# A retention + gated-convolution kernel: half of the last convolutions moved off TensorE, and the first two steps re-ordered

## The chip, the cores and the metric

The kernel runs on one core of a Trainium2 chip. The core has five engines that work beside each other, each on its own queue of instructions in a fixed order: TensorE (PE, with its weight loads shown as PEld), VectorE (DVE), ScalarE (ACT), GpSimd (POOL) and SyncE (SP, which here only issues transfers). An instruction starts when it is at the head of its queue and the semaphores it waits for have come. The metric is the device time of the launch in microseconds; less is better. The kernel before takes 191.95 us, the median of four runs (190.09 to 192.88).

## What is computed

Two stages, batch 8, 8 heads of 64, sequence 576, model width 512:

```python
# stage 1: retention, per head h with its decay gamma[h]
scores = scale * (q @ k.T)
ret    = scores * where(i >= j, gamma[h] ** (i - j), 0)
x      = (ret @ v), heads side by side           # (8, 576, 512)
# stage 2: gated unit with a causal depthwise convolution of 5 taps
gate_pre[:, t, d] = sum_k conv_w[k, d] * x[:, t + k - 4, d]
out = (sigmoid(gate_pre) * (x @ w_val)) @ w_out
```

## The kernel before, in words

**Stage 1.** The sequence of each batch element is cut into two chunks of 256 and a remainder of 64. A *step* is one 256-chunk of one element, or the remainders of two elements together; there are 20 steps, s0 to s19. The order of steps is such that a remainder step comes two steps after its pair or directly after it; the last step, s19, is a remainder. For a step, `load` brings k, q and v as f32 by SP (512 KB each for a full step), `cast` multiplies k and q with their decay factors and casts all three to bf16 (tiles `kb`, `qb`, `vb`; lines 231 and 238, on POOL except in the first two steps), `transp` turns `kb` and `qb` on PE and ACT and DVE copy the results to `kt` and `qt` (lines 251, 259, 261), `scores` makes `sc` (278) which DVE masks into `am` (285), `state` and `state_sum` keep the running state (302, 318, 320, with the bf16 copy `w` at 322), `inter` and `values` sum the step's output into the PSUM tile `o` (340, 353), and `evac` copies `o` into the stage's output `xt`, one half by DVE and one by ACT. The loads run up to four steps ahead of the step that uses them and the casts two.

**Stage 2.** When enough of `xt` is there, `push_block` (395) puts a *block* of up to 512 columns on the list `work`. The 12 blocks are, in order: two of 256 (b0), one of 512 each for b1, b2, b3, one of 256 with four remainders, 512 each for b4, b5, b6, and then two of 256 (b7) and the last four remainders. So blocks 8 to 11 have 512, 256, 256 and 256 columns. A block consists of four tiles of 128 channels (d = 0 to 3) and of these jobs:

- `conv(0)` and `conv(2)` (413): the convolution of two tiles each, as 40 matmuls with diagonal 64 x 64 weights (`diag`, made at the start by `prep_diag`, line 183), into two PSUM tiles `cps`; ACT makes the gates `gt` with a sigmoid (426);
- four `val(d)` (429): four matmuls with `w_val` into `vps` (434), then DVE multiplies with the gate into `zt` (436);
- `outp(m)` (438) for each 128 rows: four matmuls with `w_out` into `ops` (441), ACT copies to `ob` (444), SP stores it (450).

`fill(us)` takes jobs from the front of `work` while a credit lasts, so that stage 2 fills PE between the dependent pieces of stage 1. The jobs of blocks b0 (its first half) and b4 leave their `outp` on the list `late` until the next block comes.

**Order.** Nothing is scheduled automatically. Each step runs through a list of codes written out by hand: `FIRST` for s0, `SECOND` for s1, `FULL[0]` and `FULL[1]` for the other full steps, `PART` for remainders. In them `Sa`, `Sb` are scores of two head pairs each, `I` inter, `Va`, `Vb` values, `T` the transposes of the next step, `X` and `XS` the next step's state, `E` evac, `B` push_block, a number is a `fill`. In `FIRST` the step is done in two halves a and b (`first`, 477): `Ca:kD` casts half a of k on DVE, `Ca:qP` half a of q on POOL, `D2:D` and `D0:P` are `prep_diag` on DVE and POOL, `C1`, `C2` cast the steps s1 and s2, `WV`, `WO` cast the weights. After s19 the rest of `work` is emptied: this *tail* (blocks 8 to 11) has only stage 2 in it, and its `vps` and `ops` tiles take the PSUM buffers of stage 1.

Of the kernel before, what the change touches and what calls it, by code (L numbers as in the profile page):

```python
# [31 lines left out]
def kernel(  # L32
# [10 lines left out]
    nc = tc.nc  # L43
    ctx.enter_context(tc.manual_schedule())
    B, H, S, D = q.shape
    DM = moe_w_val.shape[0]
    P = 128
# [4 lines left out]
    HP = H // 2  # L52
    DT = DM // P
    KC = moe_conv_w.shape[0]
    PAD = KC - 1
    assert D == HF and DM == H * D and REM == HF and B % 2 == 0
    scale = 1.0 / math.sqrt(D)
# [1 line left out]

    TPS, DSS, CAP = False, False, 2.0  # L60
    PB, EV, TE = [4, 2, 2], "DA", "AD"
    C1, LO = "PDP", "1vo23"
    SPL, REMD = 0, [2, 0, 2, 0]
    cst = ctx.enter_context(tc.tile_pool(name="cst", bufs=1))
    ld = ctx.enter_context(tc.tile_pool(name="ld", bufs=4))
    cs = ctx.enter_context(tc.tile_pool(name="cs", bufs=4))
    at = ctx.enter_context(tc.tile_pool(name="at", bufs=3))
    sp = ctx.enter_context(tc.tile_pool(name="sp", bufs=4))
    xp = ctx.enter_context(tc.tile_pool(name="xp", bufs=2))
    gl = ctx.enter_context(tc.tile_pool(name="gl", bufs=6))  # L70
    zp = ctx.enter_context(tc.tile_pool(name="zp", bufs=2))
    os_ = ctx.enter_context(tc.tile_pool(name="os", bufs=4))
    PS = bass.MemoryType.PSUM
    scp = ctx.enter_context(tc.tile_pool(name="scp", bufs=PB[1], space=PS))
    opp = ctx.enter_context(tc.tile_pool(name="opp", bufs=PB[2], space=PS))
# [81 lines left out]
    cw = cst.tile([P, KC, DT], F32)  # L157
# [10 lines left out]


    xtb = []  # L170
    for i in range(2):
        xt_ = cst.tile([P, DT, 2, PAD + NSC * SC], BF16, tag=f"xt{i}", name="xt")
        nc.vector.memset(xt_[:, :, :, 0:PAD], 0.0)
        xtb.append(xt_)
# [43 lines left out]
    def cast(s):  # L218
        u, bb, n = steps[s]
        r = st[s]  # L220
        R = 1 if bb is None else 2
        shp = [P, R, H, D]
        f0 = n * 2
        nb = 2 if bb is None else 4
        kb = cs.tile(shp, BF16, tag=f"kb{R}", name="kb", bufs=nb)
        qb = cs.tile(shp, BF16, tag=f"qb{R}", name="qb", bufs=nb)
        vb = cs.tile(shp, BF16, tag=f"vb{R}", name="vb", bufs=nb)

        how = C1 if s == 1 else "PPP"
        for e, dst, src, f in ((how[0], kb, r["kf"], fk), (how[1], qb, r["qf"], fq)):  # L230
            (nc.vector if e == "D" else nc.gpsimd).tensor_tensor(  # L231
                dst, src.rearrange("p h r d -> p r h d"),
                f[:, f0:f0 + R, :].unsqueeze(3).to_broadcast(shp), op=ALU.mult)
        vsrc = r["vf"].rearrange("p h r d -> p r h d")
        if how[2] == "A":
            nc.scalar.copy(vb, vsrc)
        else:
            nc.gpsimd.tensor_copy(vb, vsrc)  # L238
        r.update(qb=qb, kb=kb, vb=vb)

    def transp(s, which="kq"):
        if s >= NS:
            return
        r = st[s]
        R = 1 if steps[s][1] is None else 2
        for nm in which:
            src = r[nm + "b"]
            tp = (scp if TPS else glp).tile([P, HP, R, P], BF16, tag="sc" if TPS else "gps", name="tp" + nm)
            for hp in range(HP):
                for rr in range(R):  # L250
                    nc.tensor.transpose(tp[:, hp, rr, :],  # L251
                                        src[:, rr, 2 * hp:2 * hp + 2, :].rearrange("p a d -> p (a d)"), ident)
            t = at.tile([P, HP, R, P], BF16, tag=f"{nm}t{R}", name=nm + "t")
            copy(TE[nm == "q"], t, tp)
            r[nm + "t"] = t

# [102 lines left out]
    def evac(s):  # L359
        u, bb, n = steps[s]  # L360
        r = st[s]
        R = 1 if bb is None else 2
        o = r["o"]
        if bb is None:

            if u % 2 == 0:
                xrs[u // 2] = xp.tile([P, DT, 4, PAD + REM], BF16, name="xr")
            xr = xrs[u // 2]
            j0 = 2 * (u % 2)
            nc.gpsimd.tensor_copy(xr[:, :, j0:j0 + 2, 0:PAD], xts[u][:, :, :, NSC * SC:NSC * SC + PAD])  # L370
            for x in range(2):
                copy(EV[x], xr[:, :, j0 + x, PAD:PAD + REM], o[x])
        else:
            if u not in xts:
                xts[u] = xtb[u % 2]
            for x in range(2):
                t0 = PAD + n * SC + x * P
                copy(EV[x], xts[u][:, :, bb, t0:t0 + P].rearrange("p a (i r) -> p a r i", r=R),
                     o[x].rearrange("p a (r i) -> p a r i", r=R))
        del st[s]  # L380


    work = []
    late = []
    tail = [None]

    def gps(shape, name):
# [7 lines left out]
    def push_block(xt, bi, t0, segs):  # L395


        g = {}
        z = {}
        n = segs[0][2]  # L400
        J = len(segs)
        N = n * J

        def win(d, off):
            if bi is None:
                return xt[:, d, :, off:off + n]
            return xt[:, d, bi, t0 + off:t0 + off + n]

        def fold(ap):
            return ap.rearrange("p (j t) -> p j t", j=J) if bi is None else ap  # L410

        shape = [P, N]

        def conv(d0):
            cps = [glp.tile(shape, F32, tag="gps", name="cps") for _ in range(2)]
            for kk in range(KC):
                for p2 in range(2):
                    for i in range(2):
                        for r in range(2):
                            nc.tensor.matmul(fold(cps[i][HS[r ^ i]]),  # L420
                                             lhsT=diag[HS[r], p2, kk, d0 + i, :], rhs=win(d0 + i, kk)[HS[r]],
                                             start=(kk == 0 and p2 == 0),
                                             stop=(kk == KC - 1 and p2 == 1), skip_group_check=True)
            for i in range(2):
                gt = gl.tile(shape, F32, tag=f"g{N}", name="gt")
                nc.scalar.activation(gt, cps[i], AF.Sigmoid)  # L426
                g[d0 + i] = gt

        def val(d):
            if d == 0:  # L430
                z[0] = zp.tile([P, DT, N], BF16, tag=f"z{N}", name="zt")
            vp = gps(shape, "vps")
            for do in range(DT):
                nc.tensor.matmul(fold(vp), lhsT=wval[:, do, d, :], rhs=win(do, PAD),  # L434
                                 start=(do == 0), stop=(do == DT - 1))
            nc.vector.tensor_tensor(z[0][:, d, :], g[d], vp, op=ALU.mult)  # L436

        def outp(m):
            op = gps([P, DM], "ops")
            for d in range(DT):  # L440
                nc.tensor.matmul(op, lhsT=z[0][:, d, m * P:(m + 1) * P], rhs=wout[:, d, :],  # L441
                                 start=(d == 0), stop=(d == DT - 1))
            ob = os_.tile([P, DM], F32, name="ob")
            nc.scalar.copy(ob, op)  # L444
            p0 = 0
            while p0 < P:
                col = m * P + p0
                b, tb, _ = segs[col // n]
                rows = min(P - p0, n - col % n)
                nc.sync.dma_start(out=out[b, tb + col % n:tb + col % n + rows, :], in_=ob[p0:p0 + rows])  # L450
                p0 += rows

        for d in (0, 2):
            work.append((conv, d, 0.15 + 2.15 * N / 512))
        work.extend(late)
        late.clear()
        for d in range(DT):
            work.append((val, d, 0.05 + 0.84 * N / 512))

        (work if xts[0] is not xt or bi or t0 else late).extend((outp, m, 0.9) for m in range(N // P))  # L460


    def first_tiles():
# [91 lines left out]
    for ld_ in LO:  # L555
# [4 lines left out]
        else:  # L560
# [1 line left out]
    GA, GB = list(range(HP // 2)), list(range(HP // 2, HP))  # L562
    ALL = list(range(HP))
    first_tiles()
    FIRST = ["D2:D", "Ca:kD", "Ca:qP", "Ca:vA", "Ta:qA", "Xa:", "D0:P", "Cb:kD", "Ta:kA", "Ia:", "Sa", "Tb:kD", "Cb:qP", "Cb:vP", "Xb:", "Va:", "0.0", "Ea:DD", "Tb:qA", "C1", "Wb:", "Ib:", "Tk", "Sb", "B", "Vb:", "X", "Eb:AD", "WV", "Tq", "XS", "C2", "0.0"]
    SECOND = ["1.35", "Sa", "3.3", "I", "0.9", "WO", "Sb", "Vb", "Va", "T", "4.8", "E", "X", "XS", "B", "C3", "2.45"]
    FULL = [["T", "Sa", "4.45", "X", "XS", "0.0", "I", "Sb", "4.9", "Vb", "Va", "E", "B"],
            ["Sa", "4.5", "X", "I", "XS", "Sb", "0.0", "T", "7.15", "Vb", "Va", "E", "B"]]
    PART = ["X", "XS", "1.8", "T", "I", "Sr", "6.65", "Vr", "E", "B"]
    for s in range(NS):  # L570
        u, bb, n = steps[s]
# [5 lines left out]
        for op in (PART if bb is None else FIRST if s == 0 else SECOND if s == 1 else FULL[n]):  # L577
# [20 lines left out]
                cast(1)  # L598
            elif op == "C2":
                cast(2)  # L600
            elif op == "C3":
                cast(3)
            elif op == "WV":
# [27 lines left out]
            else:  # L631
                fill(float(op))
    tail[0] = 0
    while work:
        fill(1.0)


# [28 lines left out]
```

## Time and profile before

The profiled execution is one of the four timed runs.

| what | before |
|---|---|
| median of 4 runs | 191.95 us |
| the profiled execution's own time | 190.09 us |
| its span (first to last instruction) | 188.2 us |
| mean granted TensorE clock | 0.992 |
| matmuls of stage 2 convolution, 512 wide (480) | 29.5 us busy |
| the same, 256 wide (320 + 160) | 16.3 us busy |
| POOL idle before its casts of k, waiting for the transfer of kf | 25.2 us |
| last cast of stage 1 (vb of s19) ends on POOL | 134.4 us after the start |
| first matmul of the tail | 153.43 us after the start |
| last matmul ends | about 183.4 us after the start |

The span is the time in which the core's engines had instructions; 1.9 us of the run lie around it. Rows of the profile name a line of the kernel, an engine, an operation and `out<-in` tiles. A matmul's own duration is a latency, since matmuls overlap; how long a group of them takes is read from the starts of what comes before and after it.

### The profile page before, as it was taken

To read this page: it belongs to the slowest core of one execution; us is meant where nothing else is said; L and a number is where in the kernel's file an instruction comes from. 1 tells how busy PE (TensorE), PEld (TensorE's weight loads), DVE (VectorE), ACT (ScalarE), POOL (GpSimd) and SP (SyncE) were. 2 spreads that over 40 slices of the span, in tenths; PEclk is the share of its full clock that TensorE was granted. 3 is DMA by queue.
4 is the path that set the end of the run, shared out by engine and by line. 5 is a ranking of instruction groups with operands and counts; after the bars stand their busy time and mean duration, and the time that the engine had idled before them with its cause. 6 is when DMAs were issued, how large, how long until landed. Compare 5 with 4: busy or idle time off the path is not lost.

```text
span 188.2 us, 7908 instructions
## 1 busy us (share of the span) xinstructions
PE 162.4 (86%) x3480; PEld 109.4 (58%) x3505; DVE 113.7 (60%) x212; ACT 92.8 (49%) x187; POOL 94.1 (50%) x88
## 2 busy tenths in 40 slices
PE   0176896898979998899988999989999999999990
PEld 0044784775665666565655497575855444386650
DVE  2978446389759655966497769659576801421330
ACT  6414564747442756266444675463566154254331
POOL 4997199787386867389929661885300000000000
PEclk9999999999999999999999999999999999999996
DMA  5999999999999999999999988996106041052114
GB/s 151 294 305 379 295 273 256 281 255 183 290 320 275 167 279 329 288 258 300 346 305 293 186 268 242 291 258 150 32 3 228 4 184 42 31 195 111 57 58 111
DMA packets 69039, 40.36 MB, mean 214 GB/s; under 512 B 14202, under 2 KB 63374, under 8 KB 69006
## 3 DMA queue, kind: packets, MB, share of 16 engines
q1 hardware_dynamic: 68976, 39.85, 76.9%
q8 instruction: 27, 0.44, 1.1%
q14 instruction: 6, 0.05, 0.1%
q10 hardware_dynamic: 30, 0.01, 0.0%
HBM read 30.42 MB, written 9.44 MB: 212 GB/s over the span
## 4 chain that ended last, share of the span: by engine, by line
PE 80%; DVE 9%; ACT 5%; issue 4%; ACTq 0%; DVEq 0%
PE cps L420 22%; PE ops L441 17%; PE vps L434 16%; PE tpk L251 5%; PE sc L278 5%; PE o L353 4%; PE tpq L251 4%; PE o L340 3%; DVE am L285 3%; PE ds L302 2%; ACT gt L426 2%; DVE kb L491 1%; DVE zt L436 1%; DVE diag L183 1%; DVE qt L261 1%
## 5 line engine op out<-in xcount | busy, mean ns | idle before, releaser
L231 POOL TENSOR_TENSOR kb<-kf,fk 128x1024 bf16<-128x1024 f32 (+1 forms) x19 | 33.1, 1744 | 28.6 <-DMA kf<-in_k_dram 25.2
L285 DVE TENSOR_TENSOR am<-sc,mask_c 128x512 bf16<-128x512 f32 x64 | 40.9, 682 | 6.6 <-PE sc L278 6.6
L420 PE MATMUL cps<-xt,diag 64*64 64x512 bf16 (+1 forms) x800 | 41.0, 342 | 1.8 <-DVE xt L261 1.2
L436 DVE TENSOR_TENSOR zt<-gt,vps 128x256 bf16<-128x256 f32 (+1 forms) x48 | 25.7, 552 | 24.9 <-PE vps L434 24.0
L420 PEld LDWEIGHTS <-diag 64*64 64x64 bf16 x960 | 30.5, 109 | 12.7 <-issue 4.7
L426 ACT ACTIVATE gt<-cps 128x256 f32<-128x256 f32 (+1 forms) x48 | 20.9, 488 | 27.3 <-PE cps L420 25.2
L441 PE MATMUL ops<-wout,zt 128*128 128x512 bf16 x129 | 32.8, 380 | 1.3 <-DVE zt L436 0.4
L231 POOL TENSOR_TENSOR qb<-qf,fq 128x1024 bf16<-128x1024 f32 (+1 forms) x18 | 30.8, 1711 | 3.2 <-DMA qf<-in_q_dram 3.0
L444 ACT COPY ob<-ops 128x512 f32<-128x512 f32 x36 | 20.9, 586 | 21.9 <-PE ops L441 13.5
L434 PE MATMUL vps<-xt,wval 128*128 128x512 bf16 (+1 forms) x150 | 29.4, 334 | 1.7 <-ACT xt L259 1.0
L434 PEld LDWEIGHTS <-wval 128*128 128x128 bf16 x192 | 17.5, 97 | 12.5 <-issue 1.5
L259 ACT COPY kt<-tpk 128x1024 bf16<-128x1024 bf16 (+1 forms) x19 | 17.6, 925 | 9.9 <-PE tpk L251 9.9
L441 PEld LDWEIGHTS <-zt 128*128 128x128 bf16 x144 | 12.7, 98 | 15.2 <-DVE zt L436 2.5
L238 POOL CAST vb<-vf 128x1024 bf16<-128x1024 f32 (+1 forms) x19 | 18.0, 946 | 5.8 <-DMA vf<-in_v_dram 4.3
L259 ACT CAST xt<-o 128x512 bf16<-128x512 f32 (+1 forms) x16 | 11.8, 736 | 16.1 <-PE o L353 14.5
L261 DVE COPY qt<-tpq 128x1024 bf16<-128x1024 bf16 (+1 forms) x19 | 12.0, 633 | 11.1 <-PE tpq L251 10.9
L278 PE MATMUL sc<-qt,kt 64*64 64x128 bf16 (+1 forms) x576 | 18.1, 224 | 0.1
L261 DVE CAST xt<-o 128x512 bf16<-128x512 f32 (+1 forms) x18 | 12.5, 701 | 8.0 <-PE sc L278 4.4
L322 ACT CAST w<-sn 128x256 bf16<-128x256 f32 x30 | 11.9, 406 | 7.4 <-DVE sn L318 4.4
L320 DVE TENSOR_TENSOR sn<-ds,sn 128x256 f32<-128x256 f32 x23 | 9.8, 424 | 7.4 <-PE ds L302 4.9
L353 PEld LDWEIGHTS <-vb 64*64 64x64 bf16 x544 | 9.8, 106 | 7.1 <-issue 6.6
L278 PEld LDWEIGHTS <-kt 64*64 64x64 bf16 x576 | 12.7, 110 | 1.5 <-issue 0.4
(72 smaller groups left out, 147.1 us busy)
## 6 DMA issues: line engine op xcount, KB each, us to landing
out_dram<-ob SPq DMA_DIRECT2D x32, 256.0 KB, 3.2
kf<-in_k_dram SPq DMA_DIRECT2D x15, 512.0 KB, 7.1
qf<-in_q_dram SPq DMA_DIRECT2D x15, 512.0 KB, 7.2
vf<-in_v_dram SPq DMA_DIRECT2D x15, 512.0 KB, 7.9
wvf<-in_moe_w_val_dram SPq DMA_DIRECT2D x2, 512.0 KB, 6.6
wof<-in_moe_w_out_dram SPq DMA_DIRECT2D x2, 512.0 KB, 7.5
kf<-in_k_dram SPq DMA_DIRECT2D x8, 128.0 KB, 5.9
qf<-in_q_dram SPq DMA_DIRECT2D x8, 128.0 KB, 5.2
```

The lines of the kernel that those rows point to most:

```text
L231: (nc.vector if e == "D" else nc.gpsimd).tensor_tensor(dst, src.rearrange("p h r d -> p r h d"), f[:, f0:f0 + R, :].unsqueeze(3).to_broadc ...
L238: nc.gpsimd.tensor_copy(vb, vsrc)
L259: nc.scalar.copy(dst, src)
L261: nc.vector.tensor_copy(dst, src)
L278: nc.tensor.matmul(sc[hh][HS[x], a, rj, :].rearrange("p (r i) -> p r i", r=R), lhsT=r["kt"][HS[hh], hp, rj, HS[x]], rhs=r["qt"][HS[hh], hp ...
L285: nc.vector.tensor_tensor(am, sc[hh], mk.rearrange("p j i x -> p j (i x)").unsqueeze(1).to_broadcast(shp), op=ALU.mult)
L420: nc.tensor.matmul(fold(cps[i][HS[r ^ i]]), lhsT=diag[HS[r], p2, kk, d0 + i, :], rhs=win(d0 + i, kk)[HS[r]], start=(kk == 0 and p2 == 0), ...
L426: nc.scalar.activation(gt, cps[i], AF.Sigmoid)
L434: nc.tensor.matmul(fold(vp), lhsT=wval[:, do, d, :], rhs=win(do, PAD), start=(do == 0), stop=(do == DT - 1))
L436: nc.vector.tensor_tensor(z[0][:, d, :], g[d], vp, op=ALU.mult)
L441: nc.tensor.matmul(op, lhsT=z[0][:, d, m * P:(m + 1) * P], rhs=wout[:, d, :], start=(d == 0), stop=(d == DT - 1))
L444: nc.scalar.copy(ob, op)
```

## The change

Two things are done. (1) For blocks 8 to 11 (`DV`), `conv(2)` is not put on the list. The convolution of tile 3 is done by five DVE instructions (`tap(3, k)`: multiply a shifted window by a per-channel scalar, add to an f32 accumulator), that of tile 2 by five ACT instructions that multiply and four POOL additions. `gate` makes the sigmoid: one ACT instruction for tile 2, two of 64 partitions for tile 3, whose halves are swapped. The taps of block 8 are spread over the last two full steps by the new codes `Q3` (three taps of tile 3) and `G3` (three of tile 2); those of blocks 9 to 11 are issued in the tail after `val(2)` and `val(3)` of the block before. The accumulators of tile 3 lie in PSUM in the tail. The `outp` of these blocks go on `late`. (2) `FIRST` and `SECOND` are written anew: in s0 all casts of k and q go to DVE and both of v to ACT, both `prep_diag` go to DVE, with the second after the scores; s1 is cast by POOL alone (`C1`); POOL has no work before it. `FULL[0]` has `Sa` before `T`. Besides, a third `xt` buffer takes the place of sharing the first between the batches b0, b1 and b4, b5; with it `outp` of b4 is no longer late.

```diff
-    C1, LO = "PDP", "1vo23"
+    C1, LO = "PPP", "1vo23"
+    PULL = [2, 3]
+    LATE = True
+    DV, OSB = [8, 9, 10, 11], 4
...
-    for i in range(2):
+    for i in range(3):
         xt_ = cst.tile([P, DT, 2, PAD + NSC * SC], BF16, tag=f"xt{i}", name="xt")
...
-                xts[u] = xtb[u % 2]
+                xts[u] = xtb[u % 3]
...
+    def pull(d, count):
+        for m, b in sorted(pend):
+            if b == d and pend[m, d]:
+                if all((x, d) in gated for x, y in pend if y == d and x < m - (d == 2)):
+                    for _ in range(min(count, len(pend[m, d]))):
+                        pend[m, d].pop(0)()
+                return
...
+        def tap(d, kk):
+            if kk == 0:
+                acc[d] = glp.tile([P, DM], F32, tag="gps", name="acc")[:, 0:N] \
+                    if d == 3 and tail[0] is not None else gl.tile([P, DM], F32, name=f"accs{d}", bufs=2 if d == 2 else 1)[:, 0:N]
+            if d == 2:
+                y = acc[d] if kk == 0 else gl.tile([P, DM], F32, name="prod", bufs=3)[:, 0:N]
+                nc.scalar.activation(fold(y), win(d, kk), AF.Copy, scale=cw[:, kk, d:d + 1])
+                if kk:
+                    nc.gpsimd.tensor_tensor(acc[d], acc[d], y, op=ALU.add)
+            elif kk == 0:
+                nc.vector.tensor_scalar(fold(acc[d]), win(d, 0), cw[:, 0, d:d + 1], None, op0=ALU.mult)
+            else:
+                nc.vector.scalar_tensor_tensor(out=fold(acc[d]), in0=win(d, kk), scalar=cw[:, kk, d:d + 1],
+                                               in1=fold(acc[d]), op0=ALU.mult, op1=ALU.add)
+        def gate(d):
+            while pend[me, d]:
+                pend[me, d].pop(0)()
+            gt = gl.tile([P, DM], F32, name="gt")[:, 0:N]
+            if d == 2:
+                nc.scalar.activation(gt, acc[d], AF.Sigmoid)
+            else:
+                for y in range(2):
+                    nc.scalar.activation(gt[HS[y]], acc[d][HS[1 - y]], AF.Sigmoid)
...
         def val(d):
+            if onv and d in (1, 2):
+                gate(d + 1)
...
+            if tail[0] is not None and d in PULL:
+                pull(2 if d < 3 else 3, KC)
...
-        for d in (0, 2):
+        onv = me in DV
+        if onv:
+            for d in (2, 3):
+                pend[me, d] = [(lambda kk=kk, d=d: tap(d, kk)) for kk in range(KC)]
+        for d in (0,) if onv else (0, 2):
             work.append((conv, d, 0.15 + 2.15 * N / 512))
...
-    FIRST = ["D2:D", "Ca:kD", "Ca:qP", "Ca:vA", "Ta:qA", "Xa:", "D0:P", "Cb:kD", "Ta:kA", "Ia:", "Sa", "Tb:kD", "Cb:qP", "Cb:vP", "Xb:", "Va:", "0.0", "Ea:DD", "Tb:qA", "C1", "Wb:", "Ib:", "Tk", "Sb", "B", "Vb:", "X", "Eb:AD", "WV", "Tq", "XS", "C2", "0.0"]
-    SECOND = ["1.35", "Sa", "3.3", "I", "0.9", "WO", "Sb", "Vb", "Va", "T", "4.8", "E", "X", "XS", "B", "C3", "2.45"]
-    FULL = [["T", "Sa", "4.45", "X", "XS", "0.0", "I", "Sb", "4.9", "Vb", "Va", "E", "B"],
-            ["Sa", "4.5", "X", "I", "XS", "Sb", "0.0", "T", "7.15", "Vb", "Va", "E", "B"]]
+    FIRST = ["Ca:kD", "Ca:qD", "D0:D", "Ca:vA", "Ta:kA", "Ta:qA", "Xa:", "Ia:", "Cb:kD", "Sa", "Cb:vA", "Tb:kA", "Cb:qD", "Va:", "Ea:DA", "B", "Tb:qA", "Xb:", "Ib:", "Sb", "D2:D", "1.2", "C1", "Tk", "Vb:", "Eb:AD", "Tq", "X", "XS", "1.2", "Wb:", "WV", "C2"]
+    SECOND = ["Sa", "I", "0.9", "Sb", "0.9", "Vb", "WO", "C3", "Va", "E", "B", "2.4", "T", "X", "XS", "3.0", "2.0"]
+    FULL = [["Sa", "T", "4.45", "X", "XS", "0.0", "I", "Sb", "Q3", "G3", "4.9", "Vb", "Va", "E", "B"],
+            ["Sa", "4.5", "X", "I", "XS", "Sb", "0.0", "Q3", "G3", "T", "7.15", "Vb", "Va", "E", "B"]]
```

More of the change, by code (lines that the diff above doesn't have):

```diff
@@ L61 @@
     PB, EV, TE = [4, 2, 2], "DA", "AD"
-    C1, LO = "PDP", "1vo23"
+    C1, LO = "PPP", "1vo23"
     SPL, REMD = 0, [2, 0, 2, 0]
+    VC = "P"
+    PULL = [2, 3]
+    LATE = True
+    DV, OSB = [8, 9, 10, 11], 4
     cst = ctx.enter_context(tc.tile_pool(name="cst", bufs=1))
@@ L68 @@
     sp = ctx.enter_context(tc.tile_pool(name="sp", bufs=4))
-    xp = ctx.enter_context(tc.tile_pool(name="xp", bufs=2))
+    xp = ctx.enter_context(tc.tile_pool(name="xp", bufs=1))
     gl = ctx.enter_context(tc.tile_pool(name="gl", bufs=6))
     zp = ctx.enter_context(tc.tile_pool(name="zp", bufs=2))
-    os_ = ctx.enter_context(tc.tile_pool(name="os", bufs=4))
+    os_ = ctx.enter_context(tc.tile_pool(name="os", bufs=OSB))
     PS = bass.MemoryType.PSUM
@@ L227, in cast @@
         vb = cs.tile(shp, BF16, tag=f"vb{R}", name="vb", bufs=nb)
-        how = C1 if s == 1 else "PPP"
+        how = C1 if s == 1 else "PP" + VC[s % len(VC)]
         for e, dst, src, f in ((how[0], kb, r["kf"], fk), (how[1], qb, r["qf"], fq)):
@@ L252, in transp @@
                                         src[:, rr, 2 * hp:2 * hp + 2, :].rearrange("p a d -> p (a d)"), ident)
-            t = at.tile([P, HP, R, P], BF16, tag=f"{nm}t{R}", name=nm + "t")
+            t = at.tile([P, HP, R, P], BF16, tag=f"{nm}t{R}", name=nm + "t", bufs=1 + R)
             copy(TE[nm == "q"], t, tp)
@@ L384 @@
     late = []
+    pend = {}
+    gated = set()
+    def pull(d, count):
[5 more added lines that the diff above has]
+                return
+    blk = [0]
     tail = [None]
@@ L395, in push_block @@
     def push_block(xt, bi, t0, segs):
+        me = blk[0]
+        blk[0] += 1
         g = {}
@@ L424, in conv @@
             for i in range(2):
-                gt = gl.tile(shape, F32, tag=f"g{N}", name="gt")
+                gt = gl.tile([P, DM], F32, name="gt")[:, 0:N]
                 nc.scalar.activation(gt, cps[i], AF.Sigmoid)
                 g[d0 + i] = gt
+        acc = {}
+        def tap(d, kk):
[15 more added lines that the diff above has]
+                pend[me, d].pop(0)()
+            gt = gl.tile([P, DM], F32, name="gt")[:, 0:N]
+            if d == 2:
[3 more added lines that the diff above has]
+                    nc.scalar.activation(gt[HS[y]], acc[d][HS[1 - y]], AF.Sigmoid)
+            g[d] = gt
+            gated.add((me, d))
         def val(d):
+            if onv and d in (1, 2):
+                gate(d + 1)
             if d == 0:
-                z[0] = zp.tile([P, DT, N], BF16, tag=f"z{N}", name="zt")
+                z[0] = zp.tile([P, DT, DM], BF16, name="zt")
             vp = gps(shape, "vps")
@@ L435, in val @@
                                  start=(do == 0), stop=(do == DT - 1))
-            nc.vector.tensor_tensor(z[0][:, d, :], g[d], vp, op=ALU.mult)
+            nc.vector.tensor_tensor(z[0][:, d, 0:N], g[d], vp, op=ALU.mult)
+            if tail[0] is not None and d in PULL:
+                pull(2 if d < 3 else 3, KC)
         def outp(m):
@@ L458, in push_block @@
             work.append((val, d, 0.05 + 0.84 * N / 512))
-        (work if xts[0] is not xt or bi or t0 else late).extend((outp, m, 0.9) for m in range(N // P))
+        (late if (onv and LATE) or (xts[0] is xt and not bi and not t0) else work).extend(
+            (outp, m, 0.9) for m in range(N // P))
     def first_tiles():
@@ L600 @@
                 cast(2)
+            elif op[0] == "Q":
+                pull(3, int(op[1]))
+            elif op[0] == "G":
+                pull(2, int(op[1]))
             elif op == "C3":
@@ L633 @@
     tail[0] = 0
-    while work:
+    while work or late:
+        if not work:
+            work.extend(late)
+            late.clear()
         fill(1.0)
```

## The prediction, made before the changed kernel ran

> **What bounds the kernel now.** First the page: shares by engine, and the span in 40 slices of 4.7 us.
>
> ```profile
> PE 162.4 (86%) x3480; PEld 109.4 (58%) x3505; DVE 113.7 (60%) x212; ACT 92.8 (49%) x187; POOL 94.1 (50%) x88
> ...
> PE   0176896898979998899988999989999999999990
> ...
> POOL 4997199787386867389929661885300000000000
> PEclk9999999999999999999999999999999999999996
> DMA  5999999999999999999999988996106041052114
> ...
> PE 80%; DVE 9%; ACT 5%; issue 4%; ACTq 0%; DVEq 0%
> ```
>
> PE is full from slice 4 on, at full clock; the chain that ends last is 80% PE. There are three stretches: a start of some 25 us where PE waits, a middle where PE and the transfers are both full, and a tail (from slice 33) where PE is full and POOL empty. Next the tail by blocks (columns: PE, PEld, DVE, ACT, POOL busy), one block of 256 per line:
>
> ```profile
> 165.27:171.28 6.01, 5.96 (x105) 4.30 (x106) 1.68 (x4) 2.49 (x6) 0.00 (x0) 1.00 0.34 126
> 171.28:177.28 6.00, 5.95 (x104) 4.30 (x104) 1.69 (x4) 2.49 (x6) 0.00 (x0) 1.00 0.24 90
> ```
>
> PE works 5.95 of 6.00 us while ACT has 3.5 us, DVE 4.3 us and POOL all of it free. Then the start, by the timelines of DVE, POOL and PE:
>
> ```profile
> 4.97 0.90 DVE L179 TENSOR_TENSOR cwb<-cw,cwb 128x20 bf16<-128x20 f32 x1
> 7.31 2.82 DVE L491 TENSOR_TENSOR kb<-kf,fk 128x512 bf16<-128x512 f32 x1
> 11.26 0.87 DVE L491 TENSOR_TENSOR kb<-kf,fk 128x512 bf16<-128x512 f32 x1
> ...
> 5.95 3.64 POOL L183 TENSOR_TENSOR diag<-idr,cwb 128x1280 bf16<-128x1280 bf16 x1
> 10.98 0.60 POOL L489 CAST vb<-vf 128x512 bf16<-128x512 f32 x1
> ...
> 10.19 0.43 PE L509 MATMUL ds<-vb,kb 64*64 64x64 bf16 x16 [3.69 <-DVE kb L491]
> 30.30 0.63 PE L353 MATMUL o<-am,vb 64*64 64x128 bf16 x30 [0.35 <-DVE am L285]
> ```
>
> PE waits till 10.19 for one DVE cast, which takes 2.82 us beside POOL's `diag` and 0.87 us later. In both, DVE ends 0.54 to 0.55 us after POOL's instruction does (9.59 to 10.13; 11.58 to 12.13): a half cast costs 0.55 us and the rest was blocking. Last, what feeds the middle:
>
> ```profile
> POOL kb L231 <- DMA kf<-in_k_dram: 25.2, 14, 5.6
> ...
> 42.05 1.90 POOL L231 TENSOR_TENSOR qb<-qf,fq 128x1024 bf16<-128x1024 f32 x1
> ...
> 48.09 0.61 PE L251 MATMUL tpq<-ident,qb 128*128 128x128 bf16 x8
> ```
>
> POOL waits for transfers, whose share is 9 or more until slice 23. The q of s5 is cast at 43.95 and turned on PE from 48.09: 4.1 us of slack.
>
> **Part 1, the tail: PE.** Removed are four `conv(2)`. Two convs of 512 take 153.43 to 157.88 = 4.45 us, so one 2.22; two of 256 take 2.32 (165.27 to 167.59), so one 1.16. Sum 2.22 + 3 x 1.16 = 5.7 us, all in the tail: PE's program before the tail is as long as before. PE's new tail is 2.22 conv + 3.46 val + 3.46 outp for block 8, and 1.16 + 1.85 + 1.73 = 4.74 for each of three blocks. The late `outp` only put work between gate and product.
>
> **Part 1, ACT in the tail.** Per block of 256 ACT gets 5 products, one sigmoid of 128 and two of 64 partitions in place of two sigmoids. Row: two sigmoids of 256 take 0.66 us, 0.33 each back to back, two `ob` copies 0.59 each. Sum: 5 x 0.33 + 0.66 + 3 x 0.33 + 1.18 = 4.5, and 0.28 of waiting between the two `ob` (PE makes one per 0.87): 4.8 against PE's 4.74. The Trainium skill speaks against this part: "ScalarE: Activation LUTs", What ACT_TABLE_LOAD costs, gives an ACTIVATE with immediate operands 186 ns + 0.833 ns per column, 93 ns more for each per-partition pointer operand, and 93 ns overlap back to back. A product with its scale pointer is then an estimated 0.40, the block 5.1 and ACT the bound by 0.4 us a block. No product is in this trace; the sigmoid row is near, so I take the middle: 0.2 us for each of three blocks, 0.7 with the first one's start. Ends: 0 and 1.3.
>
> **Part 1, DVE and POOL in the tail.** Five taps on a PSUM accumulator, by the `zt` row of 256 (0.42) 2.1 us; with 1.7 of `zt` 3.8 of 4.74: hidden. POOL: four additions of 256. The nearest row is the f32 product cast of 512, 1.04, so 0.52 each, 2.1 in all, made while ACT copies `ob`: hidden, up to 1.2 us for one addition.
>
> **Part 1, block 8, in s17 and s18.** There DVE is full:
>
> ```profile
> 144.46 1.29 DVE L285 TENSOR_TENSOR am<-sc,mask_c 128x512 bf16<-128x512 f32 x2 [0.96 <-PE sc L278]
> 145.66 0.42 DVE L261 COPY qt<-tpq 128x512 bf16<-128x512 bf16 x1
> 145.99 1.49 DVE L436 TENSOR_TENSOR zt<-gt,vps 128x512 bf16<-128x512 f32 x2
> ...
> 149.74 1.67 PE L441 MATMUL ops<-wout,zt 128*128 128x512 bf16 x7 [0.16 <-issue]
> ```
>
> In s18 two taps come between `am` and `qt`; behind them stand `qt`, four `zt` and `xt`, and PE's `ops` already start with the last `zt`. A tap of 512 is 0.55 (cast) to 0.68 (`am`), I take 0.6: 1.2 us on the path. In s17 three taps (1.8 us) stand ahead of `xt` and `am`, beside a conv of 2.2 us on PE: nearly covered. But these taps and POOL's additions both read two SBUF operands. The trace blocked such pairs above, and "SBUF — State Buffer", SBUF: two separate sides, says the same more strongly: the shared port pair is an exclusive lock held for the whole instruction. By the rows alone (taps at 0.6) the two steps cost 1.2; with one POOL addition of 1.04 waited for in each, 3.3. I take 1.4, since ACT's products space the additions out. ACT's own three and two products (0.54 each by the sigmoid row of 512) fall into ACT's idle time: nothing; at worst a late `xt` half, 0.5. With that cover gone, 1.6 and 1.1 us.
>
> Part 1: 5.7 - 0.7 - 1.4 = **3.6 us** gained.
>
> **Part 2, the start.** POOL is idle until k of s1 lands (by 11.5). So `cwb` is 0.18 like its neighbour; half casts are 0.55: k at 5.7, q at 6.2, `diag` (1.45) at 7.6. v on ACT as now, 7.5; `kt`, `qt` by 8.5; `ds` at 7.55 (10.19 before). The `sn` copy at 8.0, `w` 8.7, scores 9.1 (11.83 before), `am` to 11.1, values to 11.75. Second half: q cast 11.7, transposed 12.4, `qt` 13.0, scores 13.7 to 14.3, `am` 15.7, conv 14.3 to 15.5. POOL's casts of s1: k 13.6, q 15.5, v 16.5 (vf lands at 14.9 as before); its transposes on PE 15.5 and 17.0; the second `diag` waits for POOL till 16.5, ends 17.9; second conv 18.4 to 19.6. Then ACT is the queue: two `w`, two gates to 21.0, `w` 21.4, four `wval` copies (1.3) to 22.7; PE waits for the first of these 1.2 us and for the last 0.8. `val` from 22.7, and the values of s1 end at about 26.3. Before they end at 30.9 with the same work done. Gain **4.6 us**. The tight place is 11.1 to 11.5: if POOL's k cast (1.90) starts before DVE's q half, DVE stands 1.9 us longer. Ends: 2.5 and 5.5. SP's list of loads is the same and full; the loads that wait for buffers wait for casts that are not later, and two stores move ahead of the loads of s6 (one more us there, against 10 of slack).
>
> **Part 2, what the middle lets through.** Transfers do not come sooner. s5's q allows 4.1 us, and `Sa` before `T` 0.35 more (its 16 matmuls); s8 (q cast by 63.06, turned from 67.73) and s11 (82.24, 87.31) allow 4.7 and 5.1. With a little of it needed, I let **4.2** of the 4.6 arrive. From s12 on the slack is 9 us. `outp` of b4 only changes places: nothing, bounds 0.5 either way.
>
> **Sum.** 4.2 + 3.6 = 7.8. The profiled execution is 190.09 (span 188.2 and 1.9 around it), so it would be 182.3; it lies 1.86 below the median of 191.95, so **184.2 us** is my number.
>
> **Rivals.**
> - *The start is lost in the middle*: transfers hold PE back at each step, the 4.2 us become waits before s5, s8, s11. For: a transfer share of 9 in 22 slices, POOL's 25.2 us. Against: the last cast is at 134.4, its transposes at 144.34. Part 1 alone: 188.3.
> - *The tail is lost*: ACT at 0.40 a product, blocking in s17 and s18, gates late: 1.3 + 3.3 of 5.7 gone. For: full DVE rows above. Against: 14 us of idle ACT in the tail. Part 1 gives 1.1, the time is 186.6.
> - *Everything is hidden*: no DVE cost, ACT as PE: 5.7 + 4.6 (slack is enough) = 10.3, 181.7.
> - *POOL becomes the bound, slower than before*: in the tail each gate of tile 2 stands in ACT's queue ahead of the next block's products, and waits for four POOL additions in a row. The loop product - addition - gate sets the pace once an addition of 256 takes over 1.2 us. To lose 7.8 and more it has to add 2.6 us to each of three blocks, an addition of 1.8 us, 3.5 times the row; at 2.2 it is 4.2 a block, 12.6 less 7.8: 196.8. Against: no POOL row of this size is near it.
> - *The change doesn't do what it says*: the PE program has 160 matmuls fewer, 40 for each of the four blocks, so it does.
>
> **How the numbers follow.** The sum as it stands 0.60; all hidden 0.10; tail lost 0.12; start lost 0.12; POOL or another loop slower 0.06. The range 181.0 to 188.2 takes the first three and half the fourth, and the bounds of the unknown costs (products 0 to 1.3, taps 1.2 to 3.3, start 2.5 to 5.5). Within 1% (190.0 to 193.9, about what a measurement here can tell from no change) lies what start lost leaves when the tail is weak too: 0.05. Slower 0.05, faster 0.90.
>
> **What would show it.** The first `ds` at 7.6 and the values of s1 at 26; tpq of s5 near 44; the first matmul of the tail near 151 instead of 153.4; a 256 block of 4.8 to 5.0 us with ACT over 90% busy; additions of 0.5 us. I am wrong if additions are over 1.2 us, if DVE's half casts are still 0.87 or more, or if PE waits for casts in the middle.

## The result, and the profile after

The changed kernel takes 183.75 us, the median of 11 runs (181.96 to 185.39); the kernel before took 191.28 beside it (16 runs, 187.32 to 193.77). The ratio is 0.972, with a 95% interval of 0.966 to 0.977. It is taken without disturbed runs on both sides, and so is nearer to 1 than the ratio of the two medians. A second set of runs of the same kernel gave 184.1 us and 0.975 (0.969 to 0.982). So 184.2 was met, but the change itself is worth some 5 us (2.8% of 189 to 190) and not 7.8. The profiled executions say the same, with a span of 183.4 us after against 188.2 before; the one after holds a stretch at a lowered clock that cost it some 0.6. Which of the terms are too large is the question of what follows.

First the page after: busy time, four of the rows by slices of 4.6 us, the chain that ended last, and the row of POOL's casts of k.

```profile
PE 158.5 (86%) x3320; PEld 105.6 (58%) x3345; DVE 122.9 (67%) x233; ACT 106.0 (58%) x214; POOL 104.6 (57%) x101
...
PE   0579879959999998999999989799999979999980
...
ACT  6744757445551756166446746454678424989860
POOL 5069299977454968289857990876407600155420
PEclk9999999996999999999999999999999999999997
...
PE 65%; DVE 14%; ACT 10%; issue 5%; POOL 2%; POOLq 0%; ACTq 0%; DVEq 0%
...
L235 POOL TENSOR_TENSOR kb<-kf,fk 128x1024 bf16<-128x1024 f32 (+1 forms) x19 | 32.9, 1733 | 34.3 <-DMA kf<-in_k_dram 34.3
```

PE reaches its 9 in slice 3, two slices sooner, but has a 7 in slice 5 and a 5 in slice 8 (36.7 to 41.3 us); the second comes back under the middle. ACT and POOL now work in the tail (slices 34 to 37), where ACT has its highest digits. PE's share of the chain fell from 80% to 65%, and DVE's rose from 9% to 14%: there are new waits for DVE. POOL waits 34.3 us for k's transfers instead of 25.2, 9 us more, since it is now ahead of them (34.3 with the new start alone, 21.4 with the old start and the new tail). Slice 9 has a granted clock of 0.6; this comes last.

**The start.** Timelines of DVE and of PE in the changed kernel (start, duration, then in brackets the idle time before and its releaser):

```profile
5.05 0.68 DVE L551 TENSOR_TENSOR kb<-kf,fk 128x512 bf16<-128x512 f32 x1
5.66 0.68 DVE L551 TENSOR_TENSOR qb<-qf,fq 128x512 bf16<-128x512 f32 x1
6.26 1.48 DVE L187 TENSOR_TENSOR diag<-idr,cwb 128x1280 bf16<-128x1280 bf16 x1
```

```profile
6.93 0.43 PE L569 MATMUL ds<-vb,kb 64*64 64x64 bf16 x16
...
24.76 0.63 PE L357 MATMUL o<-am,vb 64*64 64x128 bf16 x30 [0.28 <-DVE am L289]
```

The half cast that had taken 2.82 takes 0.68, `ds` starts at 6.93 instead of 10.19, and the values of s1 end at about 25.4 instead of 30.9, with the same jobs done: a lead of 5.5 us.

**The middle.** PE of the changed kernel, from the scores of s2 (`sc` at 37.41) to the `ds` of s4, which is made in s3, and that of s5:

```profile
37.41 0.42 PE L282 MATMUL sc<-qt,kt 64*64 64x128 bf16 x12
39.04 0.24 PE L357 MATMUL o<-am,vb 64*64 64x128 bf16 x2 [1.20 <-DVE am L289]
39.63 0.63 PE L357 MATMUL o<-am,vb 64*64 64x128 bf16 x30 [0.35 <-DVE am L289]
40.05 0.44 PE L282 MATMUL sc<-qt,kt 64*64 64x128 bf16 x16
40.28 0.46 PE L306 MATMUL ds<-vb,kb 64*64 64x64 bf16 x32
...
49.01 0.45 PE L306 MATMUL ds<-vb,kb 64*64 64x64 bf16 x32
```

The same two `ds`, and a pause behind the second, in the kernel before:

```profile
44.37 0.45 PE L302 MATMUL ds<-vb,kb 64*64 64x64 bf16 x32
...
51.03 0.45 PE L302 MATMUL ds<-vb,kb 64*64 64x64 bf16 x32
...
52.77 0.24 PE L340 MATMUL o<-qt,w 64*64 64x128 bf16 x2 [1.11 <-issue]
```

Between the scores and the values of s2 nothing of stage 2 is left to fill the time that DVE needs for the mask. The lead is 4.1 us at the `ds` of s4 and 2.0 at that of s5.

**The last two full steps.** DVE, then POOL, of the changed kernel:

```profile
137.85 0.48 DVE L463 TENSOR_SCALAR accs<-xt,cw 128x512 f32<-128x512 bf16 x1
138.37 2.43 DVE L465 SCALAR_TENSOR_TENSOR accs<-xt,cw,accs 128x512 f32<-128x512 bf16 x2
140.93 0.73 DVE L265 CAST xt<-o 128x512 bf16<-128x512 f32 x1
...
144.53 2.42 DVE L465 SCALAR_TENSOR_TENSOR accs<-xt,cw,accs 128x512 f32<-128x512 bf16 x2
```

```profile
138.50 3.43 POOL L461 TENSOR_TENSOR accs<-accs,prod 128x512 f32<-128x512 f32 x2 [5.57 <-ACT prod L459]
143.33 3.06 POOL L461 TENSOR_TENSOR accs<-accs,prod 128x512 f32<-128x512 f32 x2 [1.41 <-ACT prod L459]
```

A tap of 512 (line 465) takes 1.22 us in the mean where I had put 0.6, in just the time in which POOL makes its additions (1.7 and 1.5 each). ACT's half of `xt` too starts only when the taps of its step are done (140.91 and 147.06), and PE waits 0.43 for the first of the two. From the `ds` made in s17 to the tail's first conv is 18.30 us (135.29 to 153.59). Before, it was 15.24 (138.19 to 153.43), but with 273 matmuls in it and not 335, since the `outp` and convs before the tail lie in other steps; a stretch with the same 335 follows with block 8 on PE.

**The tail.** The same kernel by stretches (columns as before: PE, PEld, DVE, ACT, POOL busy), one block of 256 in the second line, and then ACT and POOL in it:

```profile
165.96:170.76 4.80, 4.64 (x64) 3.29 (x64) 3.89 (x10) 4.32 (x12) 2.91 (x4) 1.00 0.23 87
170.76:175.40 4.64, 4.48 (x62) 3.11 (x63) 3.94 (x9) 4.37 (x11) 2.74 (x4) 1.00 0.18 66
```

```profile
166.04 0.51 ACT L459 ACTIVATE accs<-xt,cw 128x256 f32<-128x256 bf16 x1
166.46 1.84 ACT L459 ACTIVATE prod<-xt,cw 128x256 f32<-128x256 bf16 x4
...
167.00 2.06 DVE L465 SCALAR_TENSOR_TENSOR acc<-xt,cw,acc 128x256 f32<-128x256 bf16 x4
167.03 3.14 POOL L461 TENSOR_TENSOR accs<-accs,prod 128x256 f32<-128x256 f32 x4 [4.00 <-ACT prod L459]
...
170.21 0.42 ACT L473 ACTIVATE gt<-accs 128x256 f32<-128x256 f32 x1 [0.40 <-POOL accs L461]
```

A block has 4.80 us where it had 6.00. ACT is busy for 90% of it. ACT's own round is longer than PE's: its first product starts at 166.04 in this block and at 171.44 in the next, 5.40 us, of which 0.40 is a wait for POOL's last addition. ACT falls back by 0.6 a block, which its lead covers until the last block, where PE waits twice for `zt`, 0.25 and 0.40. The tail from its first conv (153.59) to its last matmul (about 178.6) takes 25.0 us against 30.0.

### The profile page after: what moved, and what is told of

Same layout as the page of the kernel before. It is cut to its first block, busy times and chain, and to the rows that moved or that the text cites. A ratio compares the mean times of both kernels' runs of the same rounds, so it can differ in the third digit from the quotient of the medians.

```text
span 183.4 us, 7665 instructions
## 1 busy us (share of the span) xinstructions
PE 158.5 (86%) x3320; PEld 105.6 (58%) x3345; DVE 122.9 (67%) x233; ACT 106.0 (58%) x214; POOL 104.6 (57%) x101
## 4 chain that ended last, share of the span: by engine, by line
PE 65%; DVE 14%; ACT 10%; issue 5%; POOL 2%; POOLq 0%; ACTq 0%; DVEq 0%
PE cps L439 16%; PE ops L496 15%; PE vps L487 12%; PE tpk L255 5%; DVE am L289 4%; PE o L357 4%; PE tpq L255 4%; PE sc L282 4%; ACT gt L445 3%; DVE accs L465 3%; PE o L344 2%; POOL accs L461 2%; PE ds L306 2%; DVE zt L489 2%; ACT gt L476 1%
## 5 line engine op out<-in xcount | busy, mean ns | idle before, releaser
L235 POOL TENSOR_TENSOR kb<-kf,fk 128x1024 bf16<-128x1024 f32 (+1 forms) x19 | 32.9, 1733 | 34.3 <-DMA kf<-in_k_dram 34.3
L439 PE MATMUL cps<-xt,diag 64*64 64x512 bf16 (+1 forms) x680 | 37.0, 348 | 2.3 <-issue 1.1
L439 PEld LDWEIGHTS <-diag 64*64 64x64 bf16 x800 | 26.4, 109 | 12.8 <-issue 5.2
L235 POOL TENSOR_TENSOR qb<-qf,fq 128x1024 bf16<-128x1024 f32 (+1 forms) x19 | 32.7, 1721 | 1.7 <-DMA qf<-in_q_dram 1.7
L445 ACT ACTIVATE gt<-cps 128x512 f32<-128x512 f32 (+1 forms) x40 | 17.8, 496 | 22.1 <-PE cps L439 22.0
L461 POOL TENSOR_TENSOR accs<-accs,prod 128x256 f32<-128x256 f32 (+1 forms) x16 | 15.1, 942 | 25.9 <-ACT prod L459 25.1
L263 ACT CAST xt<-o 128x512 bf16<-128x512 f32 (+1 forms) x17 | 12.3, 722 | 16.4 <-PE o L357 11.7
L282 PE MATMUL sc<-qt,kt 64*64 64x128 bf16 (+1 forms) x576 | 18.9, 223 | 0.7 <-DVE am L289 0.4
L282 PEld LDWEIGHTS <-kt 64*64 64x64 bf16 x576 | 13.5, 110 | 1.8 <-issue 1.7
(82 smaller groups left out, 178.6 us busy)
```

The source lines that it names most:

```text
L235: (nc.vector if e == "D" else nc.gpsimd).tensor_tensor(dst, src.rearrange("p h r d -> p r h d"), f[:, f0:f0 + R, :].unsqueeze(3).to_broadc ...
L263: nc.scalar.copy(dst, src)
L282: nc.tensor.matmul(sc[hh][HS[x], a, rj, :].rearrange("p (r i) -> p r i", r=R), lhsT=r["kt"][HS[hh], hp, rj, HS[x]], rhs=r["qt"][HS[hh], hp ...
L439: nc.tensor.matmul(fold(cps[i][HS[r ^ i]]), lhsT=diag[HS[r], p2, kk, d0 + i, :], rhs=win(d0 + i, kk)[HS[r]], start=(kk == 0 and p2 == 0), ...
L461: nc.gpsimd.tensor_tensor(acc[d], acc[d], y, op=ALU.add)
```

## The experiments

Each was timed beside the kernel before, and its ratio to that is given with its interval; spans and places in the trace are of one profiled execution.

**The same kernel again, and its two halves alone.**

> The changed kernel itself, to see where its time lies with TensorE at an even clock. My theory: the start is 4.1 us ahead when s4's state is made (ds of s4 near 40.3 against 44.4) and stays so up to the last full steps; there 2.1 us are given back, the tail (from its first conv to the last matmul) takes 25.0 us against 30.0. Span near 181.2. If the transfers eat the start (rival), the lead shrinks step by step to under 2 us at s17's ds (138.2 before) at an even clock too.

Measured: 0.975 (0.969 to 0.982), span 183.3. The stretch at a lowered clock came again, so the even clock that I was after is found only with block 8 on PE, below. The lead at the `ds` made in s17 is 3.0 us (135.18 against 138.19), not under 2.

Start alone: no tile leaves PE in stage 2.

```diff
-    DV, OSB = [8, 9, 10, 11], 4
+    DV, OSB = [], 4
```

> Only the second part: all convolutions stay on TensorE, the new order of the first two steps stays. My theory: 4.1 us faster than the kernel before (ratio 0.979), with the lead still there at the first conv of the tail. Rival, transfers hold the middle: 0 to 1.5 us faster (ratio 0.992 or more).

Measured: 0.983 (0.976 to 0.990), 185.31 us. The tail begins at 150.30 instead of 153.43: 3.1 us of the start's 5.5 arrive, where I had expected 4.1.

Tail alone: the lists of the first two steps, `C1` and the order of `T` and `Sa` as before.

```diff
-    C1, LO = "PPP", "1vo23"
+    C1, LO = "PDP", "1vo23"
...
-    FIRST = ["Ca:kD", "Ca:qD", "D0:D", ...
+    FIRST = ["D2:D", "Ca:kD", "Ca:qP", ...
-    SECOND = ["Sa", "I", "0.9", "Sb", ...
+    SECOND = ["1.35", "Sa", "3.3", "I", ...
-    FULL = [["Sa", "T", "4.45", ...
+    FULL = [["T", "Sa", "4.45", ...
```

> Only the first part: half of the last four convolutions off TensorE, the old order of the first two steps. My theory: the tail 5.0 us shorter and 2.1 us lost in the last two full steps, so 2.9 us faster (ratio 0.985). Rival, the additions on GpSimd and the gates hold the tail: under 1 us faster. Rival, everything hidden: 5.7 us faster (ratio 0.970).

Measured: 0.992 (0.988 to 0.996), 187.52 us, span 185.4. I had expected 2.9 us; the spans give 2.8, the times only some 1.5, and their interval ends short of 2.9. The product of the halves, 0.983 x 0.992 = 0.975, lies at the ratio of the whole, so nothing shows that they touch each other; with intervals of 0.004 to 0.007 to either side this is no proof. The 18.30 us of s17 and s18 (137.20 to 155.50) and a tail of 24.9 us are there without the new start.

**Block 8 back on PE.** Its taps in s17 and s18 go, and its second conv is made in the tail. (Three taps of block 9, half as wide, move up into s18 in their place, so that these steps are not quite without taps.)

```diff
-    DV, OSB = [8, 9, 10, 11], 4
+    DV, OSB = [9, 10, 11], 4
```

> As the changed kernel, but block 8 keeps both convolutions on TensorE, so that no tap stands in the last two full steps. My theory: TensorE gets 2.2 us more in the tail and the 2.1 us of waiting in the last two full steps go, so the time is that of the changed kernel within 0.4 us, and DVE's rows there are those of before. Rival, the waits in those steps have another cause than the taps: 2.2 us slower than the changed kernel.

Measured: 0.977 (0.970 to 0.984), no different from the whole. The stretch from s17 to the tail shrinks to 16.53 us (133.65 to 150.18), and the tail grows to 27.3. With the same 335 matmuls in both stretches, the taps of block 8 cost 1.77 us more than these three; moving its conv gains 2.3. Block 8 is hardly worth its move, as it was done.

**Products and sums apart from the taps.** GpSimd's additions of block 8 are made in s16, DVE's taps stay where they were.

```diff
-    FULL = [["Sa", "T", "4.45", "X", "XS", "0.0", "I", "Sb", "Q3", "G3", "4.9", "Vb", "Va", "E", "B"],
-            ["Sa", "4.5", "X", "I", "XS", "Sb", "0.0", "Q3", "G3", "T", "7.15", "Vb", "Va", "E", "B"]]
-    PART = ["X", "XS", "1.8", "T", "I", "Sr", "6.65", "Vr", "E", "B"]
+    FULL = [["Sa", "T", "4.45", "X", "XS", "0.0", "I", "Sb", "Q3", "4.9", "Vb", "Va", "E", "B"],
+            ["Sa", "4.5", "X", "I", "XS", "Sb", "0.0", "Q3", "T", "7.15", "Vb", "Va", "E", "B"]]
+    PART = ["G5", "X", "XS", "1.8", "T", "I", "Sr", "6.65", "Vr", "E", "B"]
```

(Both codes do nothing in the last step, so that the additions of block 9 stay in the tail.)

> Block 8's products and GpSimd additions are all made in s16, its DVE taps stay in s17 and s18. If DVE and GpSimd block each other when both read two SBUF operands (my theory), a tap of 512 falls from 1.22 to 0.55 to 0.68 us and the stretch from s17's ds to the first conv of the tail from 18.3 to 16.5 to 17.2 us; time 1.1 to 1.8 us below the changed kernel. Rival, such a tap takes 1.2 us by itself: tap and stretch unchanged, time the same.

Measured: 0.956 (0.946 to 0.966), 182.5 us. DVE of this kernel:

```profile
137.04 1.54 DVE L465 SCALAR_TENSOR_TENSOR accs<-xt,cw,accs 128x512 f32<-128x512 bf16 x2
...
142.31 1.53 DVE L465 SCALAR_TENSOR_TENSOR accs<-xt,cw,accs 128x512 f32<-128x512 bf16 x2
```

and its POOL:

```profile
127.29 5.32 POOL L461 TENSOR_TENSOR accs<-accs,prod 128x512 f32<-128x512 f32 x4 [3.49 <-ACT prod L459]
```

Same taps, same place, 0.77 us each instead of 1.22, and an addition 1.33 instead of 1.5 to 1.7. From s17 to the tail it is 16.52 us (133.97 to 150.49), as short as with block 8 on PE. Four taps at 0.45 us less are 1.8, the whole of it: the taps by themselves are hidden, and what was lost was the blocking of the two engines. (ACT's products moved with the sums; that they had part in the 1.8 is not excluded by this run alone.)

**The taps too in s16**, beside the additions.

```diff
-    PART = ["G5", "X", "XS", "1.8", "T", "I", "Sr", "6.65", "Vr", "E", "B"]
+    PART = ["G5", "X", "XS", "1.8", "T", "I", "Sr", "Q5", "6.65", "Vr", "E", "B"]
```

> All of block 8's taps, those of DVE too, are made in s16, so that s17 and s18 have none. My theory: the stretch from s17's ds to the tail is 16.5 us as with block 8 on TensorE; but five taps beside four additions and the casts of s18 stand in s16 before DVE's last copy, which gives back 0 to 2 us ahead of s17. Time 0 to 1.8 us below the changed kernel. Rival, DVE has no room anywhere: the same or slower.

Measured: 0.973 (0.965 to 0.981), the ratio of the changed kernel, and 185.95 us against 182.5 with the taps left in s17 and s18. The gain that I had expected didn't come. DVE, then PE, of this kernel:

```profile
129.45 6.37 DVE L465 SCALAR_TENSOR_TENSOR accs<-xt,cw,accs 128x512 f32<-128x512 bf16 x4
135.74 0.41 DVE L265 CAST xr<-o 128x256 bf16<-128x256 f32 x1
136.08 1.27 DVE L289 TENSOR_TENSOR am<-sc,mask_c 128x512 bf16<-128x512 f32 x2
```

```profile
136.80 0.21 PE L282 MATMUL sc<-qt,kt 64*64 64x128 bf16 x1 [2.97 <-DVE am L289]
```

Beside POOL's additions and casts a tap takes 1.59 us, the mask of s17 stands behind five of them, and PE waits 2.97. POOL suffers as well: the cast of q beside the taps takes 1.48 us, and 1.04 in the run before this. The blocking has moved with the taps; it isn't a matter of s17.

**`diag` back on GpSimd at the start.**

```diff
-    FIRST = ["Ca:kD", "Ca:qD", "D0:D", "Ca:vA", ...
+    FIRST = ["Ca:kD", "Ca:qD", "D0:P", "Ca:vA", ...
```

> The first diag is made on GpSimd again, all else as in the changed kernel. If the blocking is what held the start of the kernel before (my theory), the cast of q's first half on DVE (0.68 us in the changed kernel) stands until GpSimd's 3.6 us are over, the first ds comes near 10 us instead of 6.9, and s4's ds 1.5 to 3 us later. Rival, DVE's load set the start: DVE is free of 1.48 us, the first ds stays at 6.9 and s4's ds is the same or earlier.

Measured (one run): 186.84 us. DVE, POOL and PE of this kernel:

```profile
5.05 0.69 DVE L551 TENSOR_TENSOR kb<-kf,fk 128x512 bf16<-128x512 f32 x1
5.66 2.82 DVE L551 TENSOR_TENSOR qb<-qf,fq 128x512 bf16<-128x512 f32 x1
```

```profile
5.29 2.64 POOL L187 TENSOR_TENSOR diag<-idr,cwb 128x1280 bf16<-128x1280 bf16 x1 [1.78 <-DVE cwb L183]
```

```profile
9.07 0.43 PE L569 MATMUL ds<-vb,kb 64*64 64x64 bf16 x16
```

The half cast of q starts inside `diag` and ends 0.55 us after it, as the k cast did before. First `ds` 2.1 us later, the values of s1 2.5 later, s5's `ds` 2.3 later (50.92 against 48.58 with block 8 on PE, at an even clock). Taking work off DVE made DVE slower. One time alone decides little, but the trace does: of the start's 5.5 us, 2.5 go with this one move. How the other 3.0 divide among the rest of the new order was not tried.

**Filler kept for the next steps.** The last number of `SECOND`, a `fill` of 2.0 us, goes, so that its jobs are left for s2 and s3.

```diff
-    SECOND = [..., "2.4", "T", "X", "XS", "3.0", "2.0"]
+    SECOND = [..., "2.4", "T", "X", "XS", "3.0"]
```

> The last fill of the second step (2.0) is taken out, so that block 1's val and outp jobs lie between the dependent pieces of s2. If the part of the start's lead that is lost by s5 (5.6 us ahead at the values of s1, 2.5 us at s5's ds at an even clock) goes into waits that no stage-2 job covers (my theory), the 1.2 and 0.35 us waits for am in s2 vanish and s5's ds comes 1 to 1.6 us earlier (near 47.3 at an even clock); time 1 to 1.5 us below the changed kernel. Rival, the transfers set s4 and s5: s5's ds stays at 48.6, the wait moves to a transpose or a state product behind a GpSimd cast.

Measured: 0.955 (0.948 to 0.963), 182.38 us. PE of this kernel, at the place shown above:

```profile
35.83 0.42 PE L282 MATMUL sc<-qt,kt 64*64 64x128 bf16 x12
36.18 1.90 PE L496 MATMUL ops<-wout,zt 128*128 128x512 bf16 x7
38.01 0.69 PE L357 MATMUL o<-am,vb 64*64 64x128 bf16 x32
38.48 0.44 PE L282 MATMUL sc<-qt,kt 64*64 64x128 bf16 x16
38.71 0.46 PE L306 MATMUL ds<-vb,kb 64*64 64x64 bf16 x32
```

An `outp` now stands where PE had waited 1.20 and 0.35. Of s5 the `ds` starts at 46.87, a lead of 4.2 us, and the next ones at 56.53, 65.63, 76.11, 85.20: before they were at 61.42, 70.52, 81.00 and 90.09, so the lead is 4.9 us in all four. (The 0.7 more come from the pause of 1.11 us in the kernel before, shown above, which is not in this run.) The transfers take none of it, as POOL and PE of this kernel show for the q of s5:

```profile
40.28 1.91 POOL L235 TENSOR_TENSOR qb<-qf,fq 128x1024 bf16<-128x1024 f32 x1
```

```profile
44.14 0.61 PE L255 MATMUL tpq<-ident,qb 128*128 128x128 bf16 x8
```

The cast ends at 42.19, 1.8 us sooner than before and still 1.95 before PE needs it; the k of s5, whose cast waits for its transfer in both kernels, starts being cast at 38.42 instead of 40.19. But half of the loss in the middle is still there: from the `ds` of s4 to that of s5 it is 8.16 us (38.71 to 46.87), as in the kernel with block 8 on PE, against 6.66 before, where an `outp` at 42.76 had given DVE time. PE waits there for ACT's `xt` and DVE's `am` (0.35, 0.38 and 0.35), for s3 too has no filler.

**Both mends.** Sums apart and filler kept, together.

> The changed kernel with both mends: block 8's products and POOL sums put into s16, its DVE taps left in s17 and s18 (sums_apart), and the last fill of s1 dropped (keep_filler). Theory, that the stall in s17/s18 is VectorE and GpSimd blocking each other and the lost start lead is missing filler, two places that don't touch: the gains add, 1.8 us and 1.6 us. Span near 178.6, scores of s5 start near 46.9, the way from s17's first scores to the tail 16.5 us; ratio to the kernel before near 0.95 (0.9562 x 0.9554 over 0.973 is 0.939, from the spans 178.6/188.2 = 0.949). Rival, that the transfers or POOL's casts stand behind both: the lead gained at s5 is gone by s11 or s17 and the time is that of either mend alone, 182.4, ratio 0.956.

Measured: 0.957 (0.953 to 0.962), 181.7 us (180.13 to 182.25), span 178.4; s5's `ds` at 47.10, and 16.52 us from s17 (132.11) to the tail (148.63). By the trace the two gains add, as the theory has it: the lead over the kernel with the sums apart is still there at the `ds` made in s17 (132.11 against 133.97), and the stretch behind it is as short as in that kernel. By the times it stays open: 0.957 is the rival's number, the interval leaves out 0.949, and either mend alone (182.4 and 182.5) has an interval that holds 0.957. What is clear is that this version beats both kernels: its interval lies below that of the changed kernel.

## Why the prediction was right, and where not

| term of the sum | predicted | measured | from |
|---|---|---|---|
| start, lead at the end of s1's values | 4.6 | 5.5 | 30.9 to 25.4 |
| of it let through by the middle | 4.2 | 3.1 to 3.2 | tail of start alone; `ds` of s7 to s12 with block 8 on PE |
| tail: PE less ACT | 5.7 - 0.7 = 5.0 | 5.0 | 30.0 to 25.0 |
| taps of block 8 in s17, s18 | -1.4 | -1.8 | 18.30 against 16.53 and 16.52 |
| sum | 7.8 | 6.4 | |

- **Which way, and through which places: right.** Both halves gain, the tail by what PE loses, the start by freeing DVE from POOL's `diag` (2.5 of its 5.5 us) and by the rest of the new order.
- **The tail: the number right by luck, from two wrong sizes.** A product takes 0.51 us alone and comes every 0.42 to 0.44 in a row (166.04 and 166.46, then four up to 168.21), over both 0.33 and the estimate of 0.40; an addition of 256 is 0.73 to 0.79, not 0.52. So ACT's round is 5.40 us, and 5.0 without its wait for POOL, against PE's 4.80. The warning from the Trainium skill ("ScalarE: Activation LUTs", What ACT_TABLE_LOAD costs) was thus right about which engine is the slower one, and its 0.40 still too low. I had taken 0.2 a block where ACT falls back by 0.6, but had left ACT's lead out. The two offset each other: the loss is 0.65 us, seen at the end, for a predicted 0.7, because there are just three such blocks. The POOL rival put its point at 1.2 us an addition; at 0.79 ACT already waits 0.40 for the fourth, so by estimate that point lies near 0.7 (0.79 less a quarter of 0.40). By these numbers, more blocks of this kind would make the loop the bound.
- **The taps: the mechanism right, its size too small.** I gave the blocking 0.2 of 1.4 us, "since ACT's products space the additions out". They don't: a product comes every 0.7 us against 1.3 for an addition alone, so the additions stand back to back, and the taps between them. It was the other way round from the sum: without blocking, 0.77 a tap is hidden (nothing of the 1.2), and with it 1.8 are lost.
- **The start: term too small.** 5.5 for 4.6, though casts took 0.68 for 0.55: the second `diag` ended at 17.1 and not 17.9, since it waited less for POOL, and the first `val` started at 21.6 and not 22.7.
- **The middle: the wrong step.** "s5's q allows 4.1 us", hence "I let 4.2 of the 4.6 arrive", made transfers the cap. They were not: "transfers do not come sooner" is false (with filler kept, the k of s5 lands 1.8 us sooner), and they let 4.9 through. What took 2.3 of the 5.5 was on PE: the new `SECOND` spends its fills in s1, and s2 and s3 then have nothing between scores and values. The lead falls from 5.5 to 4.1 at the `ds` of s4 and to 2.5 at that of s5 (at an even clock), some 1.5 us in each of s2 and s3; the later 3.2 is this 2.5 and the pause in the kernel before. I had counted what `SECOND` issues, and not what it uses up. With those jobs kept, s2's part comes back: s5 starts 1.7 us sooner, and its q is turned at 44.14 (I had said near 44; 46.28 in the changed kernel). That s3's part has the same cause is argued from its waits and was not tried. PE waiting for casts, the sign that I had named against the middle, never came. The first matmul of the tail, forecast near 151, stands at 153.59 for this reason and the one above.
- **The sum.** 6.4 by these terms, 4.8 between the two profiled executions. Of the 1.6 between, 0.6 is the lowered clock below (8.73 us from s4's `ds` to s5's, 8.16 with block 8 on PE) and 0.9 one stretch before s17 (115.66 to 126.66, 11.00 us, against 10.10 with block 8 on PE and the same work), in which PE pauses 1.08 for nothing that the profile shows. Such pauses are in the trace of before too, at other places; what they are was not tried. The hit of 184.2 is thus partly luck: it owes 2 to 3 us to the median that I subtracted from. 183.75 over 0.972 is 189, where I started from 191.95.

## What to carry to other kernels

Work handed to another engine isn't free for the first: before VectorE and GpSimd get a share each, look whether the two will run at the same time on SBUF operands, and put one of them a step earlier rather than both side by side. When a start is made faster, list what fills the gaps between dependent pieces in the steps after it: a fill that is spent sooner comes back as a wait two steps on, and dropping it can gain. A stretch of a few blocks can be run beyond the pace of its second engine, if that engine starts ahead; reckon the lag times the number of blocks and not the rate.

## What the runs showed of the hardware

**Blocking goes both ways.** A VectorE tap of 512 takes 0.77 us alone, and 1.22 to 1.59 in the mean beside GpSimd (single taps of the changed kernel 0.74 to 1.64); a GpSimd addition of 512 takes 1.33 alone and up to 1.7 beside VectorE. The prediction drew on the Trainium skill for a lock between the two engines ("SBUF — State Buffer", SBUF: two separate sides), and the runs agree with it: with `diag` on GpSimd, VectorE's cast begins at 5.66, inside `diag`, and ends 0.55 us after it, 2.82 us where it takes 0.68 alone. It matters where the operands lie. A tap of 256 whose accumulator lies in PSUM takes 0.49 us beside the additions of the tail, all twelve of them. With block 8 on PE, two taps of 256 with the accumulator in SBUF take 0.83 each beside additions (in s18) and two 0.48 without any (in the tail).

**A stretch at half clock.** In the changed kernel (and with its start alone) the granted clock falls for some 3.5 us. Stretches of 1 us, the clock third from the end:

```profile
41.00:42.00 1.00, 0.90 (x17) 0.82 (x17) 1.00 (x3) 0.05 (x1) 1.00 (x2) 0.59 1.11 365
42.00:43.00 1.00, 0.94 (x22) 0.60 (x18) 0.87 (x4) 0.40 (x1) 1.00 (x1) 0.50 1.01 259
43.00:44.00 1.00, 1.00 (x12) 1.00 (x11) 1.00 (x3) 0.53 (x2) 1.00 (x2) 0.50 0.32 74
44.00:45.00 1.00, 1.00 (x35) 0.80 (x36) 0.54 (x2) 0.89 (x1) 0.04 (x1) 0.71 0.63 143
```

and with block 8 on PE, whose program is the same up to there:

```profile
42.00:43.00 1.00, 0.63 (x20) 0.54 (x20) 0.87 (x3) 0.32 (x1) 1.00 (x2) 1.00 1.12 264
```

Matmuls take nearly twice as long in it (the eight transposes of `tpk` take 0.83 us up to the first of `tpq`, 42.80 to 43.63, and 0.46 in the next step, 45.82 to 46.28). Three profiles show it (the changed kernel twice, its start alone), and three with the same program up to there don't (block 8 on PE, sums apart, taps early); unprofiled runs of the changed kernel had mean clocks from 0.985 to 0.999. What sets it off stays open; no run here was made for it.
